# Sketched attention and a gated expert attention on one core: the same jobs in another order

## The chip, the core and the metric

The kernel runs on one core of a Trainium2 chip. The metric is device time in microseconds for one execution, as the median of several; lower is better. The core has five engines that work beside each other, each through its own queue in a fixed order: TensorE (matmuls, PE in the profile), VectorE (DVE), ScalarE (ACT), GpSimd (POOL) and SyncE (SP, which here only starts DMA transfers). An instruction that waits for a semaphore stops everything behind it in its engine's queue.

## What is computed

Two blocks, one after the other, in float32, for 4 batches (`b`) of 1088 positions. Cut to what matters:

```python
# block 1, per batch and head (4 heads of 32)
a, b = x @ S1.T, x @ S2.T                  # 8 sketches each, for q and for k
phi  = outer(a, b)                         # 64 features
kv, z = phi(k).T @ v, phi(k).sum(0)
x = (phi(q) @ kv) / (phi(q) @ z + 1e-6)    # heads side by side: x is 1088 x 128
# block 2: 4 experts, the best 2 of them per position
logits = x @ w_gate
w = softmax over the best 2 logits
for e in experts:
    s = causal((x @ wq[e]) @ (x @ wk[e]).T / 8)
    out += w[e] * softmax(s) @ (x @ wv[e]) @ wo[e]     # where e is among the best 2
```

## The kernel before, in words

The kernel does not walk through loops at run time. It first makes a list of 1275 jobs (`job(...)`, line 79 on): each has a name, one or two engines that it may run on, the values that it reads and makes, the buffers that it holds, and a function that issues its instructions. The constant `ORDER` then names every job once, by its number; a letter behind the number chooses the engine (`a` the first, `b` the second; for the dummy matmuls that warm TensorE up, `b` leaves them out). `Plan.run` (line 85 on) takes the words one after the other:

```python
for word in order:
    n, a = (int(word[:-1]), "ab".index(word[-1])) if word[-1] in "ab" else (int(word), 0)
    j = self.jobs[n]
    ...
        for h in j["holds"]:
            if h not in self.where:
                self.where[h] = free[h[0]].popleft()
        j["f"](j["eng"][a])
```

So `ORDER` decides three things: how the instructions of each engine stand in its queue, which of two engines does a job, and which buffer of a pool a value gets (the one longest free). The framework adds the semaphore waits that the data and the buffers need. Costs written beside the jobs (`us`, `landing`, `rank`) do nothing at run time; the order was found with them outside this file. `mode` is the tile shape in which a job uses TensorE's array: F for 128 x 128 tiles, V for 32 x 128, Q for 32 x 32, M for 128 x 64, L for 128 x 32, and two more for small jobs.

The jobs by stage, with the names that the prediction uses and their lines in the profile:

- Start: 6 dummy matmuls (line 248, two each); loads of S1, S2, q, k, v and the weights; `decode` (303 to 315, VectorE) makes float32 of the sketch matrices, whose inputs come as float64, and `spread1` to `spread3` copy them to the four blocks of 32 partitions.
- Block 1 of batch 0: `turn q0.x` and `turn k0.x` (transposes, 485 and 481); `sketch q0`, `sketch k0` (TensorE, 516); `back ...` (VectorE transposes out of PSUM, 520); `features ...` (products of two sketches, 525, on VectorE or GpSimd); `turn qf` (TensorE, 590), `sums 0.m` (556), `numer 0.m` (613), `divide` (620 to 622), `turn x` (628), `keep x`. Later batches use other steps of the same kind (`sketch`, `back`, `weigh q`, `invert q`, `scale q`, `features`, `turn f`, `numer`, 734 to 768), prepared while the batch before is in block 2. `repeat S2` (352) is a small TensorE job for them.
- x goes to DRAM (`store x`, 640 and 645 for batch 0) and comes back in another layout (`fetch x`, 649 and 786) as weights for the later sums.
- The choice of experts: `logits` (806), `choose a`, `choose b` (831 to 847, small comparisons of two SBUF operands on VectorE), `turn choice` (885, 887), `shares` (GpSimd, 865 to 881); masks for three groups of columns go through DRAM (`store masks`, `fetch masks`, 891 and 896), those of the very first group come by `widen` and `keep mask`.
- Block 2 goes by 3 groups of 64-row steps (6, 6 and 5 steps of 17; a step takes 64 positions with the two experts chosen). Per group: `query` (TensorE, 959), `base` and `pick` (972). Per step i: `score b.i` (997), `take` (adds the mask and finds the maximum, VectorE, 1009), `exp` (ScalarE, 1025), `guard` (1031 or 1033), `invert` (1036), `weigh` (GpSimd, 1040), `turn A` (VectorE transpose, 1045). Per group again: `sum` (TensorE, 1073), `keep V`, `patch V` (1096), `spread V` (GpSimd, 1100), `out` (1144, 1170, 1194), `turn out`, `keep out`, `store out`.

All TensorE results pass through 4 PSUM buffers of two banks (`pair0` to `pair3`), so a score waits until an earlier `take` or `keep` has read the buffer that it gets. Copies (line 192) can run on ScalarE or VectorE.

Of the kernel before, what the change touches and what calls it, by code (L numbers as in the profile page):

```python
# [21 lines left out]
0 3 45 1 42a 16a 8a 5a 22a 26b 2 46 77 7b 48 49 88 76 4 52 51 74 75 56 21a 87 85 86 50 96 78 98 101b 79 53 102a 82 97  # L22
100b 99a 54 64 89 90 27b 81 80 10b 84b 65 92b 66 83a 393 394 91 95b 67a 107 108a 60 111 392 93a 115 109 116a 113 19b
103 112a 13b 110a 63 114a 94a 104 58 391 402 401 405 406 408a 407 395 404 106a 105a 29b 121 122 399 117 118 398 125
123 126 44b 119 403 55 400 397 57 120a 124b 127 685 396 128a 687 59 61 62a 68 70 409a 686 148 131 410a 149 150 146 151
167 147 69 168 411a 152 153 170 154 412 413 414a 684 694 155 132 130 415 133 179 129 171 172 135 180 183a 24b 416 417
420b 418b 419b 162 695 184a 163 164 156 157a 158 159a 181 12b 182 421 185 186 187 194 422 423 47 195 196 424 425 246
188 201 430 426 165 166a 71 202 169 245 431 197a 73 198 189 190b 199 191 192 432 427a 428b 72 215 216 200 250a 174
433a 247 222 249a 251 223 224 225a 208 209 203 193 217 434a 210 211b 25b 248 318 319 322a 252 175 429 160 226 204a 173
689 260 261 691 227 435 212 213 161a 690 253 254 323a 324 14b 214 228 176 218a 219 220 140 436 255 688 437a 136 438a  # L30
205 206 698 699 700 704a 177 320 207 267 256a 702a 134 321 325 221 268 262 263a 264 178a 265 269 270 697 284 283 285
701a 291 292 293 456 458 137 229 230 271a 286 231 141 294 235a 234a 696 287b 295a 257 703b 457 258 272 692 273 693 705
461 459 460 296 31b 232a 236 297 706 143 233b 707a 275 708 462 238 709 710 711a 463 288 289 276 237 239 259 712a 266
277 342 274 278 343 344 144 345 298 279b 280 290 281 713a 714 715 717 716 723 346a 347 348 327 326 38b 328 472 473 329
282 724 725 476a 718 477b 464 478 467 719 350 351 352 726a 353 439 299 300 330b 331 332 727a 349 301 139 138 302 303
304 308a 333 441 142 354a 307b 306b 9b 17b 35b 335 310 474 440 334 305b 309 475 336 479 359 337 338a 358 360 339 361
362 355 468 508 509 442 720a 984 311 312 540 721a 363 340 501 364a 443 502 480 979 341 481 482 541 314 465 487 365 488
356 357 483a 315 313 366 367 538 494 977 978 495 980 316a 981 728 539 542a 368 369 370 987 496 503 504a 145 371 372
373 374 317 469 375 470 543a 544 545 471a 505 506 985 988 484 485 486 497b 444 498 722 499 510 511b 489 490a 491 512
513 376 379b 447 500 380a 515 383 516 553 377a 381 445 554 492 493 378a 382 448 584 585 586 517 518a 729 555 449 446  # L40
453 982 983 730a 514 519 731b 451 991 520 521 993 749 556b 992 994b 587 588a 569 546 996b 750 384 385 997a 507 557 558
547 751 548 386 568 989 522 589 523 524 549a 550 551 559 570 571 526a 752 753 590 242 591 525a 754 611 529 995a 530
241 528b 527a 531 612 616a 561 760 732 452 387 615a 755 455 466 733 572a 756 560 573 574 389 614 562 563 986 613 240
576 577 617 618 620 575 43b 552 532 644 619 578 28b 18b 579 621 243a 580b 581 643 765 652 564a 565 766 769a 582 651
768 757 645 583 636 566 567 390 653 770a 771 635 654 655 627 622 244 623a 761 762 628 637 656 657b 629 630 638 767 772
624 658 659 646 625 592 660 639a 640 631b 641 593 594 450 595 596 597 794 598a 999 647a 632 642 601b 602 648 600a 599a
795 633 634 649 998 736 1000a 603 605 535 626 454 773 774 787 650 534 763 788 533 780 781 808 809 810 811a 764a 536b
812 661 662 789 775 663 813 796 797b 798 790b 604 782 664 665 666 667 1002 814 668 669 990 1005a 734 776b 777 672a
671a 778 1006b 670b 1001 735 739 1003 832 1004a 791 388 799 783b 800 673a 674 675 831 835a 801 784 1007 802 803 1008
792 676 1009 793 836a 834 677 1010 1016 833 904 738 678 742 758 804b 1011 837 30b 1017 785 805 806 759 1012 1018 838  # L50
1013a 905 908a 862 1014a 1020a 909a 807 679 910 878 786 779 737 537 877 879 747 839 840 841 907 906 880 911 861 863
1019a 1021 881b 842a 846 847 682 740 815 816 817 746 864 865a 820a 853 866 867 821a 824 854 1015 868 882 936 819a 823
855 39b 34b 40b 41b 848 849b 937 818a 850 851 856 822 938 1022 1024b 869 1023b 607 843 883 884 939 870 748 871 872
1042 857b 1044 928 680 741 681 844 845 1043 858 606 873a 874 929 608 1045 825 1047 852 930 940a 1046 1048 875 859 860
921 944 945 946 920 743 941 609a 922 610 744 913 931 932a 1049 912 914 947 933 934 942 915 948 876 949 950b 1131 916a
# [1228 lines left out]
```

## Time and profile before

| | |
|---|---|
| Time, median of 3 runs | 273.25 us (273.1 to 274.25) |
| Span of the profiled execution | 272.5 us |
| TensorE busy | 261.4 us, 4081 matmul instructions |
| VectorE busy | 215.1 us |
| GpSimd busy | 153.9 us |
| ScalarE busy | 102.0 us |
| HBM traffic over the span | 98 GB/s |

The span runs from the first to the last instruction; the rest of a run's time lies around it. A float32 matmul appears as two instructions. TensorE's ends are modelled and overlap the next start, so spacing between starts says more than a duration. In the timeline a line has its start, the time to the end of the last of the merged instructions, engine, line of the kernel, operation, what it writes and reads, shape, count, and in brackets the idle time ahead of it with what ended that. Lines of the DMA view have the count, the size and the median time from issue to landing.

### The profile page before, as it was taken

How to read it: one execution, taken by the hardware profiler on the slowest of the kernel's cores; microseconds unless marked ns; L12 is line 12 of the kernel's file. 1: busy time of each engine (PE TensorE's matmuls, PEld its weight loads, DVE VectorE, ACT ScalarE, POOL GpSimd, SP SyncE). 2: the span in 40 equal slices, each digit the busy share in tenths (PEclk: the TensorE clock that was granted, in tenths of full speed). 3: DMA queues.
4: the chain of work that ended last, by engine and by line, in shares of the span. 5: the costliest groups of instructions: out<-in, count | busy, mean ns of one | idle time of the engine just before them, and what ended most of it. 6: DMA issues, size and time to landing. Idle time of an engine off the chain costs nothing.

```text
span 272.5 us, 9727 instructions
## 1 busy us (share of the span) xinstructions
PE 261.4 (96%) x4081; PEld 194.4 (71%) x4081; DVE 215.1 (79%) x534; ACT 102.0 (37%) x274; POOL 153.9 (56%) x248
## 2 busy tenths in 40 slices
PE   7789999989999999989999999999999999999994
PEld 2578754557596895766599976756696975789994
DVE  4878789889999879998968438999899368995244
ACT  2052346643423517143552341453433335334110
POOL 3498179757679545545574558565448342653640
PEclk9999999999999999999999999999999999999999
DMA  6869569921638979045700166601502755830012
GB/s 203 144 129 148 124 124 179 194 30 30 132 65 141 210 183 165 17 89 108 162 6 4 38 146 153 159 1 39 110 2 71 140 119 119 168 76 2 5 31 53
DMA packets 80588, 27.38 MB, mean 100 GB/s; under 512 B 49760, under 2 KB 79520, under 8 KB 80544
## 3 DMA queue, kind: packets, MB, share of 16 engines
q1 hardware_dynamic: 80096, 26.10, 49.0%
q8 instruction: 32, 0.52, 0.8%
q10 hardware_dynamic: 448, 0.66, 0.7%
q14 instruction: 12, 0.10, 0.1%
HBM read 22.22 MB, written 4.52 MB: 98 GB/s over the span
## 4 chain that ended last, share of the span: by engine, by line
PE 73%; DVE 14%; DMA 6%; issue 3%; ACT 1%; POOL 1%; SPq 1%; DVEq 0%
PE pair L1073 27%; PE pair L997 21%; PE pair L959 8%; PE pair L1194 6%; PE pair L556 2%; DMA xra<-xd 2%; PE pair L1144 2%; DMA in<-in_k_dram 2%; DVE fp L525 2%; DVE w L520 2%; PE pair L516 2%; DVE w L1009 1%; DVE AT L1045 1%; PE pair L1170 1%; PE pair L756 1%
## 5 line engine op out<-in xcount | busy, mean ns | idle before, releaser
L1040 POOL TENSOR_SCALAR w<-w,rs,sh 128x384 f32<-128x384 f32 (+15 forms) x68 | 56.9, 844 | 56.2 <-DVE rs L1036 53.9
L1025 ACT ACTIVATE w<-w,mx 128x384 f32<-128x384 f32 (+15 forms) x68 | 52.4, 771 | 72.0 <-DVE mx L1009 64.8
L997 PE MATMUL pair<-xT,qs 128*128 128x384 f32 (+11 forms) x216 | 76.1, 480 | 2.8 <-DVE agg L192 1.3
L997 PEld LDWEIGHTS pair<-xT,qs 128*128 128x128 f32 x216 | 37.7, 190 | 28.8 <-issue 10.7
L1045 DVE STREAM_TRANSPOSE AT<-w 128x576 f32<-128x576 f32 (+15 forms) x68 | 50.9, 759 | 6.1 <-POOL w L1040 5.5
L1009 DVE CUSTOM_DVE_ANT_0 w<-pair,mask 128x768 f32<-128x768 f32 (+14 forms) x68 | 48.2, 719 | 6.4 <-PE pair L997 5.9
L1073 PEld LDWEIGHTS pair<-AT,xra 32*128 32x128 f32 x1136 | 41.3, 185 | 5.8 <-DVE mx L1009 2.6
L1073 PE MATMUL pair<-AT,xra 32*128 32x160 f32 (+5 forms) x1136 | 44.2, 302 | 0.0
L1100 POOL TENSOR_TENSOR agg<-agg,mb 128x768 f32<-128x768 f32 (+1 forms) x22 | 34.1, 1560 | 10.7 <-ACT agg L192 4.5
L959 PE MATMUL pair<-xT,Mq 128*128 128x384 f32 (+1 forms) x96 | 35.0, 477 | 0.1
L525 POOL TENSOR_TENSOR fp<-w 128x576 f32<-128x576 f32 x24 | 28.9, 1219 | 6.9 <-DVE w L520 6.9
L192 ACT COPY agg<-pair 128x384 f32<-128x384 f32 (+1 forms) x32 | 13.7, 461 | 42.1 <-PE pair L1073 34.5
L1073 PE MATMUL pair<-AT,xrb 32*128 32x160 f32 (+5 forms) x752 | 26.8, 287 | 0.1
L1073 PEld LDWEIGHTS pair<-AT,xrb 32*128 32x128 f32 x752 | 26.1, 185 | 0.7 <-issue 0.7
L972 DVE COPY_PREDICATED qs<-mb,pair 128x768 f32<-128x768 uint16 (+1 forms) x24 | 23.1, 961 | 2.6 <-DMA mb<-md 1.3
L959 PEld LDWEIGHTS pair<-xT,Mq 128*128 128x128 f32 x96 | 17.2, 190 | 10.4 <-issue 2.5
L1194 PEld LDWEIGHTS pair<-Mo,agg 128*128 128x128 f32 x168 | 20.6, 192 | 2.4 <-issue 1.3
L1194 PE MATMUL pair<-Mo,agg 128*128 128x128 f32 x168 | 21.6, 278 | 0.0
L192 DVE COPY agg<-pair 128x384 f32<-128x384 f32 (+1 forms) x14 | 7.5, 536 | 12.7 <-PE pair L1073 7.5
L1036 DVE RECIPROCAL rs<-rs 128x1 f32<-128x1 f32 x68 | 8.9, 141 | 8.1 <-POOL rs L1033 6.3
L1033 POOL TENSOR_SCALAR rs<-zs 128x1 f32<-128x1 f32 x30 | 6.4, 214 | 15.7 <-ACT w L1025 12.8
L1096 DVE COPY_PREDICATED agg<-mb,pair 128x384 f32<-128x384 uint16 (+1 forms) x24 | 12.7, 547 | 3.2 <-ACT agg L192 3.0
(159 smaller groups left out, 307.5 us busy)
## 6 DMA issues: line engine op xcount, KB each, us to landing
mb<-md SPq DMA_DIRECT2D x7, 576.0 KB, 5.3
xra<-xd SPq DMA_DIRECT2D x16, 192.0 KB, 4.8
xrb<-xd SPq DMA_DIRECT2D x16, 192.0 KB, 4.1
xrc<-xd SPq DMA_DIRECT2D x16, 160.0 KB, 4.1
mb<-md SPq DMA_DIRECT2D x4, 480.0 KB, 5.4
in<-in_k_dram SPq DMA_DIRECT2D x12, 136.0 KB, 4.2
in<-in_q_dram SPq DMA_DIRECT2D x3, 544.0 KB, 5.6
xd<-w SPq DMA_DIRECT2D x12, 136.0 KB, 3.5
```

What stands on the lines that cost most here:

```text
L192: (nc.scalar.copy if eng == "ACT" else VEC[eng].tensor_copy)(o, i)
L525: VEC[e].tensor_tensor(out=f, in0=a[:, :, None, R : 2 * R].to_broadcast([128, NJ, R, R]), in1=a[:, :, 0:R, None].to_broadcast([128, NJ, R, ...
L959: nc.tensor.matmul(plan[ps[x]][:, y, 0:w], Mq[:, ((1, 2), (0, 3))[x][y]], plan[xT][:, 64 * t0 : 64 * t1], start=True, stop=True)
L972: nc.vector.copy_predicated(chosen(), rows(c), rows(plan[ps[x]]))
L997: nc.tensor.matmul(plan[p][:, y, 0 : c1 - c0], plan[qs][:, 128 * t : 128 * t + 128], plan[xT][:, c0:c1], start=True, stop=True)
L1009: nc.vector.tensor_tensor_reduce(out=o, in0=src, in1=msk, scale=-1.0, scalar=mx[:, b, i, x - 1 : x] if x else 3e38, op0=ALU.add, op1=ALU.m ...
L1025: nc.scalar.activation(out=a, in_=a, func=ACTF.Exp, bias=mx[:, b, i, last : last + 1], scale=-1.0, accum_out=zs[:, b, i : i + 1])
L1040: nc.gpsimd.tensor_scalar(out=a, in0=a, scalar1=rs[:, b, i : i + 1], scalar2=plan[("sh", b)][:, i : i + 1], op0=ALU.mult, op1=ALU.mult)
L1045: nc.vector.transpose(dst[:, 0 : keys // 32, t], plan[A][:, 0:keys].rearrange("p (j s) -> p j s", s=32))
L1073: nc.tensor.matmul(plan[Vk[g // 2]][:, g % 2, lo : 32 * nt], plan[(f"xr{j // 12}", b)][rows, j % 12], a[rows, j, lo:], start=(j == 0), sto ...
L1100: nc.gpsimd.tensor_tensor(out=a, in0=a, in1=plan[mb][:, 2 * x : 2 * x + 2, 0:w], op=ALU.mult)
L1194: nc.tensor.matmul(plan[p][0:m, 0, 128 * x : 128 * x + 128], plan[agg][:, e, 128 * x : 128 * x + m], Mo[:, e], start=(e == 0), stop=(e == ...
```

## The change

Only `ORDER` is replaced. The jobs, their instructions and their sizes stay; every job is still there once, with the same six pairs of dummy matmuls. The first and last lines of both lists:

```diff
 ORDER = """
-0 3 45 1 42a 16a 8a 5a 22a 26b 2 46 77 7b 48 49 88 76 4 52 51 74 75 56 21a 87 85 86 50 96 78 98 101b 79 53 102a 82 97
-100b 99a 54 64 89 90 27b 81 80 10b 84b 65 92b 66 83a 393 394 91 95b 67a 107 108a 60 111 392 93a 115 109 116a 113 19b
...
-1260 1262a 1100 1195 1264a 1085 1196 1197 1199 1263b 1261a 1265 1266 1268 1198 1072 1086 1108 1109 1267 1200a 1201
-1110 1115b 1116 20b 1269 1111a 23b 1113 1112 1119 1114b 1270 1273 1271 1117 1118b 1274 1120 1121 1122 1272 1127b 1128b
-1123b 1124a 1125b 1126a 36b
+0 3 1 76 2 79 77 87 45 5a 48 4 75 78 8a 22a 42a 74 88 16a 56 51 21a 86 60 50 46 80 54 49 81 85 52 53 96 82 97 89 98 59
+57 392 90 101a 61 65 393 62a 66 100b 391 102a 91 99b 18b 64 83a 94a 111 115 67a 84a 116a 95a 92b 394 93a 58 109 107 113
...
+1267 1198 1111a 1268 1200a 1112 1201 1113 1269 1115a 974 1116 1114a 1117 1119 1118b 1120 13b 1121 1270 1122 1271 1273
+1127b 1274 1125a 1272 1126b 1128a 1123a 1124b
 """.split()
```

By names, the engines' queues at the places that the prediction speaks of (old above new):

```
SP, start
 old  load S0, q0.0, w0, k0.0, w4, v0.0, v0.1, w1, v0.4, w2, v0.3, v0.2 ...
 new  load q0.0, S0, v0.1, v0.0, k0.0, w4, v0.2, w2, v0.3, w0, w1, v0.4 ...
VectorE, start
 old  decode, turn q0.1, spread3, turn q0.0, turn k0.0, turn k0.1, back q0.1, features q0.3, back q0.0,
      features q0.0, back k0.0, back k0.1, features k0.1, features k0.2, turn k1.1, turn k1.0, back k1.0 ...
 new  turn q0.0, decode, turn q0.1, spread3, turn k0.1, turn k0.0, back q0.0, back q0.1, back k0.0, features q0.2,
      features q0.3, back k0.1, features k0.2, features k0.3, features k0.1, turn k1.1, turn k1.0, keep sums 0.0 ...
GpSimd, start
 old  features q0.2, features q0.1, spread v1, features k0.0, features k0.3, pick8, onehot, rep4, features k1.0 ...
 new  rep16, gate order, features q0.1, features q0.0, features k0.0, rep4, onehot, features k1.3 ...
TensorE, start
 old  sketch q0, turn w0, sketch k0, turn w1, turn w2, turn qf, sums 0.0, sums 0.1, sketch k1, numer, turn x, repeat S2 ...
 new  sketch q0, sketch k0, repeat S2, turn w1, turn w2, turn w0, turn qf, sums 0.1, sums 0.0, sketch k1, numer, turn x ...
SP, around the stores of x
 old  ... load k2.1, v1.0, k2.3, k2.2, store x 0.2, load k2.0, store x 0.3, 0.1, 0.4, 0.0, store masks 0, fetch masks 0.1 ...
 new  ... load k2.2, k2.0, k2.3, store x 0.4, 0.2, 0.3, 0.1, 0.0, load k2.1, fetch x 0.02, store masks 0, fetch x 0.12 ...
VectorE, around sum 1.0
 old  ... take 1.9.0, choose a2.0, choose b2.0, turn A 1.11, maximum 2.0, patch V 1.0.0, patch V 1.0.1, keep V 1.0.1 ...
 new  ... take 1.9.0, choose a2.0, maximum 2.0, take 1.6.0, back k3.0, choose b2.0, base 1.2.1, pick 1.2.0 ...
```

Of the 1241 jobs that are issued, 86 change engine: 5 go from VectorE to GpSimd and 4 the other way (7 of these 9 are feature products), 21 copies go from VectorE to ScalarE and 16 the other way, 37 `guard` and spread jobs change between ScalarE and GpSimd, and three stores of the last group change between SP and ScalarE. TensorE's 314 jobs have 65 changes of tile shape between neighbours in the new list, 69 in the old.

More of the change, by code (lines that the diff above doesn't have):

```diff
@@ L27 @@
[L27 to L55, printed above, removed]
-917 951 1130 1053 918 1054 1129 1133b 935 1025 1132 923 952 885 886 943 887 888 889 890 1134a 1051 891a 1135 1136 892b
```

56 lines of the change are left out of this document (43 added, 13 removed).

## The prediction

> **What bounds the kernel now.** I read the page's first part, then the windows by stage, then TensorE's timeline around its gaps, and last what VectorE and GpSimd did there.
>
> ```profile
> span 272.5 us, 9727 instructions
> PE 261.4 (96%) x4081; PEld 194.4 (71%) x4081; DVE 215.1 (79%) x534; ACT 102.0 (37%) x274; POOL 153.9 (56%) x248
> ```
>
> ```profile
> 0.00:20.00 20.00, 16.36 (x400) 10.05 (x403) 14.09 (x31) 6.13 (x12) 11.29 (x29) 1.00 0.71 162
> 20.00:37.00 17.00, 16.52 (x284) 12.62 (x279) 14.04 (x49) 5.26 (x13) 9.18 (x22) 1.00 0.66 118
> 37.00:57.00 20.00, 18.11 (x196) 10.16 (x183) 18.12 (x51) 11.41 (x36) 16.99 (x34) 1.00 1.10 171
> 57.00:92.00 35.00, 35.00 (x524) 25.44 (x523) 32.77 (x82) 13.32 (x35) 26.16 (x34) 1.00 0.47 89
> 92.00:124.00 32.00, 30.68 (x566) 23.86 (x565) 28.93 (x70) 13.10 (x39) 15.50 (x26) 1.00 0.64 126
> 124.00:262.00 138.00, 137.69 (x2048) 106.28 (x2050) 102.56 (x243) 52.28 (x141) 73.86 (x108) 1.00 0.37 80
> 262.00:272.50 10.50, 7.01 (x98) 5.96 (x90) 4.56 (x11) 0.48 (x1) 0.88 (x1) 1.00 0.23 55
> ```
>
> The columns are TensorE, its weight loads, VectorE, ScalarE and GpSimd, then clock, DMA share and GB/s. TensorE is the bound: from 57 us to 262 us it idles 1.6 us in all, and the granted clock is 1.00 throughout. Its jobs are the same in both lists, so an order can win only four things: waits (3.6 us of idle before 20 us, 1.9 us between 37 and 57, 1.3 us between 92 and 124), the cost of tile shape changes, work placed where TensorE waits anyway, and the end. VectorE is a close second from 20 to 92 us, with 64.9 us busy of 72.
>
> **The price of a shape change.**
>
> ```profile
> 86.78 0.81 PE L959 MATMUL pair<-xT,Mq 128*128 128x384 f32 x2
> 87.42 0.76 PE L997 MATMUL pair<-xT,qs 128*128 128x256 f32 x4
> 143.15 0.70 PE L997 MATMUL pair<-xT,qs 128*128 128x256 f32 x2
> 143.78 2.29 PE L556 MATMUL pair<-vp,fp 128*64 128x33 f32 x72
> ```
>
> Modelled ends overlap, so I take start to start. A 384-column pair among its like is 0.64 us, so 256 columns are 0.43. The score at 143.15, with a change before and a change behind it, takes 0.63: half of each change falls into it, so one change is 0.2 us.
>
> **TensorE's list against its time.** The spacing of each kind of job, where it waits for nothing, summed over the two lists, with 0.2 per change:
>
> ```profile
> 24.85 0.82 PE L628 MATMUL pair<-ident,w 128*128 128x128 f32 x6
> 58.99 3.18 PE L1073 MATMUL pair<-AT,xra 32*128 32x192 f32 x92
> 266.10 2.92 PE L1170 MATMUL pair<-Mo,agg 128*128 128x128 f32 x24
> ```
>
> From the last numerator of batch 0 (ended 24.85) to the first `sum` (58.99) the old list holds 27.5 us of jobs and 19 changes, 31.3 us; it took 34.1, so 2.8 us are waits. From there to the last output block (266.10) it holds 196.7 us and 43 changes, 205.3; it took 207.1, so 1.8 us are waits. The new list holds 28.2 us with 21 changes (32.4) and 195.4 us with 38 changes (203.0). Together 236.6 becomes 235.4: **-1.2 us**, of which 0.6 are three changes saved here (69 to 65 over the whole list) and 0.6 is `repeat S2`, which moves ahead of the numerators into time in which TensorE waits for features. If that cover were gone, its 0.6 would come back.
>
> **The wait at 119.9 us.**
>
> ```profile
> 114.78 1.68 POOL L1040 TENSOR_SCALAR w<-w,rs,sh 128x448 f32<-128x448 f32 x2 [1.21 <-DVE rs L1036]
> 115.94 0.59 DVE L831 TENSOR_TENSOR ch<-ch 128x34 f32<-128x34 f32 x1
> 116.42 1.18 POOL L525 TENSOR_TENSOR fp<-w 128x576 f32<-128x576 f32 x1
> 116.45 1.23 DVE L832 TENSOR_TENSOR ch<-ch 128x34 f32<-128x34 f32 x1
> 117.80 0.21 DVE L835 TENSOR_TENSOR ch<-ch 128x34 f32<-128x34 f32 x1
> 120.60 0.54 DVE L192 COPY agg<-pair 128x384 f32<-128x384 f32 x1
> 121.19 1.24 PE L997 MATMUL pair<-xT,qs 128*128 128x288 f32 x4 [1.32 <-DVE agg L192]
> ```
>
> `choose a2.0` on VectorE has two instructions that take 0.59 and 1.23 us instead of 0.21, each ending where a GpSimd instruction ends: GpSimd holds VectorE for 1.4 us. Everything behind in VectorE's queue is late by that, the copy at 120.60 (`keep V 1.0.1`) last, and TensorE waits 1.32 us for the PSUM that it frees. The new list gives that copy to ScalarE, puts `choose a2.0` behind another `take`, and puts score 1.8 before `sum 1.0.0`. Late next is `sum 1.0.0`: from score 1.9.00 to it, back, choices, base and two picks keep VectorE 6.2 us against 5.8 us of TensorE work, 0.4 us short. Net **-0.9** (0 if a new hold falls there, -1.3 if none).
>
> **Up to the numerators.**
>
> ```profile
> 2.88 0.17 DVE L303 TENSOR_SCALAR w<-w 32x32 int32<-32x32 int32 x1 [1.62 <-DMA w<-in_S_dram]
> 4.18 0.23 DVE L315 STREAM_TRANSPOSE SK<-w 32x64 f32<-32x64 f32 x1
> 5.74 0.78 DVE L485 STREAM_TRANSPOSE in<-in 128x576 f32<-128x576 f32 x1 [1.33 <-DMA in<-in_q_dram]
> in<-in_q_dram SPq DMA_DIRECT2D x1, 256.0 KB, 3.5
> 6.58 0.77 PE L516 MATMUL pair<-in,SK 32*32 32x32 f32 x64
> 7.54 1.50 PE L516 MATMUL pair<-in,SK 32*32 32x256 f32 x64 [0.19 <-DVE in L485]
> 12.75 1.43 DVE L520 STREAM_TRANSPOSE w<-pair 128x576 f32<-128x576 f32 x2
> 14.06 2.31 POOL L525 TENSOR_TENSOR fp<-w 128x576 f32<-128x576 f32 x2
> 14.11 3.54 DVE L525 TENSOR_TENSOR fp<-w 128x576 f32<-128x576 f32 x2
> 41.05 0.74 DVE L525 TENSOR_TENSOR fp<-w 128x576 f32<-128x576 f32 x1
> ```
>
> The new list loads q0.0 first on SP (issue at about 1.0, landing 3.5 later, 4.5) and puts `decode` (13 instructions, 2.88 to 4.4, so 1.5 us) behind its turning: 4.5 + 0.7 + 1.5 + 0.8 for `turn q0.1` + 0.2 for the spread lets the first sketch begin at 7.7 instead of 6.6. The two v loads put ahead of k0.0 on SP make k0.0 later too, but by 10.1, when this sketch (2.4 us) ends, it need not be there before. The next sketch then runs straight on, in PSUM of its own, to 12.4; so `back k0.0` starts at 12.4, not 12.75. Behind it stand five feature products on VectorE (one more than was there) and a turning: 0.72 + 5 x 0.74 + 0.7 = 5.1, done at 17.5 if nothing holds them; in the old list they were done at 17.65, with 3.54 us for two, 2.1 over the free price. GpSimd now runs its three products, the copies of rep4 and the one-hot beside them, so a hold is likely here: between none and two products (2.3 us). I take one, 1.15, against the 0.2 won: **+0.9** (-0.2 to +2.2).
>
> The Trainium skill (SBUF — State Buffer, Who interferes with whom) says that a VectorE instruction with two SBUF inputs and a GpSimd instruction that reads SBUF exclude each other for a whole instruction, whichever starts first. By that alone a hold ends with the GpSimd instruction in flight, and the sum would be the one I take; the row at 14.11 waited for two in a row, and by that row it would be 1.2 us worse.
>
> **From the numerators to the first sum.**
>
> ```profile
> 26.13 1.99 SPq L640 DMA_DIRECT2D xd<-w  x1
> 30.91 0.42 SPq L640 DMA_DIRECT2D xd<-w  x1
> in<-in_k_dram SPq DMA_DIRECT2D x12, 136.0 KB, 4.2
> 34.75 2.18 DVE L972 COPY_PREDICATED qs<-mb,pair 128x768 f32<-128x768 uint16 x2
> 36.62 6.97 SPq L440 DMA_DIRECT2D vp<-in_v_dram  x3
> 37.13 1.45 DVE L520 STREAM_TRANSPOSE w<-pair 128x576 f32<-128x576 f32 x2 [0.21 <-PE pair L516]
> ```
>
> The last load of k2 moves behind all stores of x on SP. These ran from 26.13 to 31.3 with one load among them; without it they end at 30.8, and the load lands 4.2 later, at 35.0. `turn k2` waits for it, and on VectorE's queue stand behind it the first picks, `back q1` and the first takes: 35.0 + 1.5 + 2.2 + 0.2 + 1.45 + 0.5 for `take 0.4.0` is 40.8. Score 0.1.00 needs that take's PSUM; TensorE's work ahead of it since 24.85 is 14.4 us, 39.3. So the new list waits 1.5 us there; the chains behind it, to `sum 0.0.0`, are shorter than TensorE's work. With 0.1 for the rest, 2.8 becomes 1.6: **-1.2** (-2.2 to +1.0).
>
> **Elsewhere** no chain of the new list between TensorE steps is more than 0.2 us longer than TensorE's work beside it; but many are only just shorter, so I keep 0 with -0.5 to +1.5. The end (turn out, three copies, stores split otherwise over ScalarE and SP) has the same number of steps: 0, within 0.3.
>
> **Sum**: -1.2 - 0.9 + 0.9 - 1.2 = -2.4; 272.5 - 2.4 = 270.1. The median of the runs shown, 273.25, is 0.75 above the span, so the forecast is **270.8 us**.
>
> **The rivals.** *Held twice at the start*: the feature products lose 2.3 us to GpSimd and the wait at 119.9 shrinks by half only; +1.1 and +0.5 make it 272.4. For it speaks the row at 14.11, against it that two of GpSimd's three products can run there before VectorE's first is ready. *No holds at all*: the start gains 0.2 instead of losing 0.9, the wait at 119.9 goes whole (-1.3), and the sum is -3.9, 269.3. For it: VectorE hands five copies more to ScalarE than it gets back, 2.7 us less work at the 0.54 of the row at 120.60; against it: one feature product more at the start. *SP's queue sticks* (the slower side): at 36.62 three loads kept SP for 6.97 us. If the new list's queue sticks so before the last k2 load, which now lies behind five stores, that load lands up to 5.5 us later (7.0 less the 1.4 that the first store already shows above the others), and VectorE and TensorE with it: 270.8 + 5.5 - 0.5 of waits swallowed is 275.8. It decides from 3.8 us of lateness on. Against it: the old queue was free again by 28.2. *The change buys nothing*: the changes saved are real, but chains with no slack give it back; 273.0.
>
> **How the numbers follow.** Forecast 0.47, no holds 0.15, held twice 0.16, nothing bought 0.10, queue sticks or another slower end 0.12. Half a per cent, about what a measurement can tell here, is 1.4 us: faster is below 271.9, slower above 274.6. Forecast (its own range 269.8 to 272.1, nine tenths faster) and no holds make 0.58 faster; the rest of the forecast, held twice and nothing bought 0.30; slower 0.12. The range reaches from the best bounds that come together (268.4) to most of the queue's case (274.8).
>
> **What would show it.** Right: TensorE's idle time in 92 to 124 us below 0.6; the first numerators ending between 24.6 and 27; VectorE's `L831`/`L832` near 0.2 us; TensorE's first `sum` near 59.8 (58.99 + 0.9 - 1.2, and 1.1 more work ahead of it). Wrong: `L525` on VectorE far above 0.74 before 20 us, a VectorE wait for k2's load longer than 2 us, or new TensorE idle behind 124 us, where the old list has 0.3.

## The result, and the profile after

| | before | after |
|---|---|---|
| Time, median (20 runs each) | 273.37 us | 275.91 us |
| Ratio, 95% interval | | 1.009 [1.0069, 1.0111] |
| Span of the profiled execution | 272.5 us | 273.9 us |
| Time of the profiled execution | not told | 275.64 us |

The new order is slower by 2.5 us; forecast were 270.8 us, between 268.4 and 274.8. In all 20 runs of the changed kernel the time is 1.7 to 1.8 us above the span. The clock below is the granted TensorE clock, as a share of full speed. The page of the kernel after, its first part:

```profile
span 273.9 us, 9738 instructions
PE 263.2 (96%) x4081; PEld 197.0 (72%) x4081; DVE 210.4 (77%) x528; ACT 104.7 (38%) x280; POOL 156.2 (57%) x248
```

The same stretches as before, of the kernel after (length, then TensorE, its weight loads, VectorE, ScalarE, GpSimd, clock, DMA share, GB/s):

```profile
0.00:20.00 20.00, 16.14 (x296) 10.46 (x296) 13.07 (x30) 6.22 (x12) 11.69 (x33) 0.84 0.75 167
20.00:37.00 17.00, 16.75 (x316) 13.82 (x316) 12.70 (x48) 5.48 (x15) 7.16 (x13) 0.99 0.59 111
37.00:57.00 20.00, 19.87 (x252) 11.36 (x251) 19.61 (x51) 11.06 (x34) 16.18 (x34) 1.00 1.00 166
57.00:92.00 35.00, 34.71 (x514) 24.49 (x514) 33.40 (x85) 14.44 (x38) 26.26 (x35) 1.00 0.63 122
92.00:124.00 32.00, 31.20 (x573) 23.86 (x572) 23.37 (x66) 13.07 (x39) 15.60 (x30) 1.00 0.43 82
124.00:262.00 138.00, 136.43 (x2082) 105.93 (x2080) 104.92 (x246) 52.50 (x141) 76.53 (x106) 1.00 0.42 82
```

Three things catch the eye. Before 20 us the clock is 0.84 (1.00 before) and TensorE got 296 matmuls done instead of 400. From 20 to 57 us TensorE no longer waits: 0.4 us of idle time against 2.4. Behind 57 us its idle time is larger, 2.7 us against 1.6, and most of that is behind 124 us (1.6 against 0.3), where I had forecast none.

TensorE's timeline of the kernel after, from the dummies to `turn qf` (its number of matmuls is behind the x, the idle time ahead of it in brackets):

```profile
1.31 5.30 PE L247 MATMUL pair<-idle 128*128 128x512 bf16 x12 [1.31 <-DVE idle L240]
6.82 3.14 PE L515 MATMUL pair<-in,SK 32*32 32x32 f32 x211 [0.20 <-DVE in L484]
12.30 1.33 PE L515 MATMUL pair<-in,SK 32*32 32x256 f32 x45 [2.34 <-issue]
13.56 1.06 PE L351 MATMUL pair<-ident,rep 32*128 32x32 f32 x4
14.55 1.54 PE L379 MATMUL pair<-ident,AT 128*128 128x128 f32 x6
15.88 4.31 PE L589 MATMUL pair<-ident,fp 128*128 128x128 f32 x18
```

In the middle of the second sketch, at 10 us, TensorE stops for 2.34 us, and the reason given is "issue": it waits for nothing that the profile shows. No semaphore stands there. What ends shortly before is a DMA that no instruction of the kernel starts. The DMA view of before between 8.5 and 9 us:

```profile
q1 hardware_dynamic: 66, 0.02, 26.0%
q8 instruction: 1, 0.02, 18.0%
```

and of after between 9.5 and 10 us (between 6 and 9.5 us it has no such line, and q1 is at 113.8%):

```profile
q1 hardware_dynamic: 403, 0.09, 126.4%
q8 instruction: 1, 0.02, 16.3%
```

Over the whole run of the kernel after, this queue shows:

```profile
q8 instruction: 32, 0.52, 0.8%
```

That is 32 pieces of 16 KB for the 8162 instructions that the page counts on TensorE (4081 matmuls and as many weight loads), 255 to a piece: I take q8 for the queue of TensorE's own instructions. In the new list the piece begins a us later, with the DMA engines full of the kernel's loads (q1's packets take 126% of that half microsecond, 26% before). It takes 1.3 us (16.3% of 16 engines' half microsecond), and TensorE goes on about 1.4 us behind its end. Since it now does both sketches in one run, TensorE gets to the place where it stops 1.6 us sooner than in the old list: it stops behind a matmul that began at 9.6, and the old list began that one at 11.2 us.

Behind the stop the clock falls. Windows of the kernel after:

```profile
12.00:14.00 2.00, 1.70 (x47) 1.12 (x47) 0.83 (x2) 0.00 (x0) 0.04 (x1) 0.89 1.01 160
14.00:20.00 6.00, 6.00 (x27) 5.32 (x27) 5.97 (x6) 4.50 (x9) 5.57 (x6) 0.50 0.50 134
20.00:22.00 2.00, 2.00 (x61) 1.88 (x62) 1.71 (x3) 0.00 (x0) 0.00 (x0) 0.90 0.00 0
```

0.89, 0.50 and 0.90 make half clock from 13.6 to 20.4 us, 6.8 us long; the 18 matmuls of `turn qf` take 4.31 us in it. The Trainium skill (TensorE: Matmul & The Clock Gate, Part 1) has the gate pass half of the pulses after an idle window of about 3.4 us. The half clock is there, twice as long as that; but TensorE stood still for only 2.34 us.

VectorE and GpSimd of the kernel after, beside it:

```profile
13.17 0.78 DVE L519 STREAM_TRANSPOSE w<-pair 128x576 f32<-128x576 f32 x1 [2.85 <-PE pair L515]
13.88 2.37 DVE L524 TENSOR_TENSOR fp<-w 128x576 f32<-128x576 f32 x2
16.98 3.45 DVE L524 TENSOR_TENSOR fp<-w 128x576 f32<-128x576 f32 x3
14.03 1.60 POOL L524 TENSOR_TENSOR fp<-w 128x576 f32<-128x576 f32 x1 [1.99 <-DVE w L519]
15.58 2.31 POOL L343 COPY rep<-ident 32x128 f32<-32x128 f32 x4
17.96 1.86 POOL L367 CAST AT<-ident 64x1536 bf16<-64x1536 f32 x1
```

`back k0.0` waits 2.85 us for the sketch. The five feature products behind it take 2.37 + 3.45 = 5.82 us where 5 x 0.74 = 3.70 were free: they are held by GpSimd for 2.1 us, all along `features k0.0`, `rep4` and `onehot`. They end at 20.4, the moment at which `turn qf` at half clock ends too (20.2): the two delays lie side by side.

**Stage by stage**, on the spans (starts of the first `turn x`, of the first `sum` and of the last output block; the fourth line is the run of the old start with the new rest, the last the kernel before, profiled again):

| | to turn x | to first sum | to last out | to the end | span |
|---|---|---|---|---|---|
| before | 24.85 | 34.14 | 207.1 | 6.4 | 272.5 |
| forecast | 25.75 | 34.05 | 203.9 | 6.4 | 270.1 |
| after | 28.05 | 31.83 | 207.1 | 6.9 | 273.9 |
| old start, new rest | 24.79 | 32.52 | 207.1 | 7.1 | 271.5 |
| before, again | 24.86 | 33.06 | 207.0 | 6.5 | 271.4 |

### The profile page after: what moved, and what is told of

Same layout as the page of the kernel before. It is cut to its first block, busy times and chain, and to the rows that moved or that the text cites. A ratio compares the mean times of both kernels' runs of the same rounds, so it can differ in the third digit from the quotient of the medians.

```text
span 273.9 us, 9738 instructions
## 1 busy us (share of the span) xinstructions
PE 263.2 (96%) x4081; PEld 197.0 (72%) x4081; DVE 210.4 (77%) x528; ACT 104.7 (38%) x280; POOL 156.2 (57%) x248
## 4 chain that ended last, share of the span: by engine, by line
PE 85%; DVE 7%; issue 2%; ACT 2%; DMA 2%; POOL 1%; ACTq 0%; DVEq 0%; POOLq 0%
PE pair L1072 27%; PE pair L996 24%; PE pair L958 9%; PE pair L1193 6%; PE pair L515 5%; PE pair L1143 3%; PE pair L555 3%; DVE AT L1044 2%; DMA in<-in_q_dram 2%; PE pair L612 2%; PE pair L589 1%; PE pair L805 1%; DVE qs L971 1%; ACT agg L191 1%; DVE agg L1095 1%
## 5 line engine op out<-in xcount | busy, mean ns | idle before, releaser
L1039 POOL TENSOR_SCALAR w<-w,rs,sh 128x64 f32<-128x64 f32 (+14 forms) x68 | 56.0, 829 | 53.2 <-DVE rs L1035 45.9
L996 PE MATMUL pair<-xT,qs 128*128 128x320 f32 (+11 forms) x216 | 75.1, 479 | 2.3 <-DVE qs L971 0.7
L1024 ACT ACTIVATE w<-w,mx 128x768 f32<-128x768 f32 (+16 forms) x68 | 52.4, 771 | 49.4 <-DVE mx L1008 42.2
L1072 PEld LDWEIGHTS pair<-AT,xra 32*128 32x128 f32 x1136 | 42.4, 185 | 4.5 <-DVE AT L1044 1.2
L1072 PE MATMUL pair<-AT,xra 32*128 32x160 f32 (+5 forms) x1136 | 45.1, 302 | 0.0
L524 POOL TENSOR_TENSOR fp<-w 128x576 f32<-128x576 f32 x25 | 29.5, 1195 | 12.1 <-DVE w L519 11.7
L1072 PEld LDWEIGHTS pair<-AT,xrb 32*128 32x128 f32 x752 | 26.7, 185 | 0.2 <-issue 0.2
L191 ACT COPY qs<-pair 128x384 f32<-128x384 f32 (+1 forms) x20 | 8.8, 463 | 17.5 <-PE pair L958 17.4
L515 PE MATMUL pair<-in,SK 32*32 32x288 f32 (+2 forms) x544 | 12.5, 356 | 2.7 <-issue 2.3
```

The source lines that it names most:

```text
L191: (nc.scalar.copy if eng == "ACT" else VEC[eng].tensor_copy)(o, i)
L515: nc.tensor.matmul(dst if early else dst.rearrange("p (j t) -> p j t", t=32), SK[rows, 1] if s else first_[rows], part(src[rows], g), star ...
L524: VEC[e].tensor_tensor(out=f, in0=a[:, :, None, R : 2 * R].to_broadcast([128, NJ, R, R]), in1=a[:, :, 0:R, None].to_broadcast([128, NJ, R, ...
L996: nc.tensor.matmul(plan[p][:, y, 0 : c1 - c0], plan[qs][:, 128 * t : 128 * t + 128], plan[xT][:, c0:c1], start=True, stop=True)
L1024: nc.scalar.activation(out=a, in_=a, func=ACTF.Exp, bias=mx[:, b, i, last : last + 1], scale=-1.0, accum_out=zs[:, b, i : i + 1])
L1039: nc.gpsimd.tensor_scalar(out=a, in0=a, scalar1=rs[:, b, i : i + 1], scalar2=plan[("sh", b)][:, i : i + 1], op0=ALU.mult, op1=ALU.mult)
```

## The experiments

Each ratio is to runs of the kernel before on the same chip; it is an estimate over the single executions and not the quotient of the medians, so where executions spread the two differ. The kernel before against itself gave 1.0027 (below), so a third of a per cent is not told apart by times alone. Each kernel was profiled in one execution only; what is read from its timeline holds for that one.

**Which part of the list costs.** Two halves, joined at the last `turn x` of batch 0:

```diff
 e1: order = old[:112] + [w for w in new if w not in old[:112]]
 e2: order = new[:110] + [w for w in old if w not in new[:110]]
```

> The old list's first 112 words (up to the last turn x of batch 0), then the rest in the new list's order. Theory A (the start costs: TensorE ran out of instructions at 10 us in the new list because the two sketches of 256 small matmuls each stand next to each other, and the idle window then halved its clock): no idle time of TensorE over 1 us before 20 us, granted clock 1.00 from 7 us on, numerators of batch 0 done at 25.0 +- 0.4 instead of 28.2, first sum between 57.0 and 58.8 instead of 59.9, time 1.5 to 2.8 us below the changed kernel's 275.9. Rival B (the start's lateness is swallowed later, the loss stands in the new list's many small waits behind 60 us): numerators at 25 too, but first sum at 59.5 to 60 and a time within 0.6 us of 275.9.

Measured: 273.37 us, 0.9976 [0.9955, 0.9997]. The first `turn x` begins at 24.79, the first `sum` at 57.31, the clock is 1.00.

> The new list's first 110 words (up to the last turn x of batch 0), then the rest in the old list's order. Theory A: the gap of 2.3 us at 10 us and the half clock from 13.6 to 20.4 us are there again, numerators done at 28.2, first sum between 60 and 61.5 instead of 59.0, time 0.8 to 2.2 us above the kernel before (274.2 to 275.6). Rival B: the same gap and clock, but the first sum at 59.0 to 59.5 and a time within 0.6 us of the kernel before.

Measured: 276.77 us, 1.0097 [1.0062, 1.0131]. The gap is there again (TensorE's timeline of e2):

```profile
7.33 3.14 PE L515 MATMUL pair<-in,SK 32*32 32x32 f32 x211 [0.72 <-DVE in L484]
12.00 1.33 PE L515 MATMUL pair<-in,SK 32*32 32x256 f32 x45 [1.53 <-issue]
```

So the start makes the whole loss, 2.5 us with the new rest and 3.2 with the old one (1.2 us beyond what I gave it, and its first sum, at 62.3, is later than I gave it too; why the old rest makes it dearer is not shown). The rest of the new list is worth 0.2% by the ratio and nothing by the medians (273.37 against 273.52 beside it), less than the kernel before differs from itself: theory A holds, and rival B is right in that the new rest does not win what it should.

**Is it code that TensorE waits for?** The dummy matmuls are cut smaller, so that more instructions stand ahead in TensorE's queue:

```diff
-nc.tensor.matmul(plan[h][:, 0], idle[:, 0:128], idle, start=True, stop=True) for _ in range(2)]
+nc.tensor.matmul(plan[h][:, 0, 0:128], idle[:, 0:128], idle[:, 0:128], start=True, stop=True) for _ in range(7)]
```

> The new list; each of the six dummy jobs issues 7 matmuls of 128 columns instead of 2 of 512, so TensorE's queue holds 60 instructions more ahead of the first sketch, in about the same time. If TensorE's gap at 10 us is a wait for instructions (theory A), it is tied to the place in TensorE's instruction stream: it begins 15 float32 matmuls (30 matmul records) earlier in the second sketch, 0.2 to 0.4 us sooner, and the third piece of code starts to load that much sooner too. If it is a wait for k0's data or for VectorE (rival C), the gap ends at the same matmul of the second sketch as in the changed kernel. Time within 0.8 us of 275.9 by both.

Measured: 276.04 us, 1.0082 [1.0054, 1.011]. TensorE's timeline of e3:

```profile
1.31 4.66 PE L247 MATMUL pair<-idle 128*128 128x128 bf16 x42 [1.31 <-DVE idle L240]
6.90 3.62 PE L515 MATMUL pair<-in,SK 32*32 32x32 f32 x181 [0.92 <-DVE in L484]
12.59 1.96 PE L515 MATMUL pair<-in,SK 32*32 32x32 f32 x57 [2.08 <-issue]
```

42 + 181 = 223 matmuls stand ahead of the gap, as 12 + 211 = 223 in the changed kernel and in e2. The gap moved by exactly the 30 records, to a matmul that in the changed kernel ran without a wait. That speaks against data, PSUM and the other engines, which stand at places in the data: the gap stands at a place in TensorE's code. One part of the expectation failed: the piece did not load sooner (it began at 10.0) and the gap did not begin sooner, since the first sketch itself came a little later; so it is not the using up of the earlier code alone that sets the piece's time.

**Filling the gap.** Four dummies more between the sketches:

```diff
-... sketch q0, load v0.4, back q0.0, sketch k0 ...
+... sketch q0, load v0.4, back q0.0, dummy, dummy, dummy, dummy, sketch k0 ...
```

> The new list with four more dummy jobs (eight bf16 matmuls of 512 columns, 0.21 us each at full clock, 1.7 us together) between the two sketches. Theory A: the code comes at the same time, so the second sketch still ends at 13.6 +- 0.4, but TensorE's idle time is only 0.5 to 1.2 us, the clock stays 1.00, the 18 matmuls of turn qf take 2.4 us instead of 4.3, and the numerators are done at 26.6 +- 0.5; if that reaches the end, the time is 274.3 to 275.3, by rival B 275.5 to 276.2. Rival C (data): the gap keeps its length and stands 1.7 us later, numerators no earlier than 28.

Measured: 276.97 us, 1.0113 [1.007, 1.0156]. TensorE's timeline of e4:

```profile
1.31 4.20 PE L247 MATMUL pair<-idle 128*128 128x512 bf16 x12 [1.31 <-DVE idle L240]
6.73 2.04 PE L515 MATMUL pair<-in,SK 32*32 32x32 f32 x128 [1.22 <-DVE in L484]
8.70 2.13 PE L247 MATMUL pair<-idle 128*128 128x512 bf16 x8
10.76 1.21 PE L515 MATMUL pair<-in,SK 32*32 32x32 f32 x75
12.31 1.40 PE L515 MATMUL pair<-in,SK 32*32 32x256 f32 x53 [0.35 <-issue]
16.75 2.22 PE L589 MATMUL pair<-ident,fp 128*128 128x128 f32 x17 [1.56 <-DVE fp L524]
```

12 + 128 + 8 + 75 = 223 again, and the next matmul at 12.31, as with the gap unfilled: the code came no sooner. The second sketch ended at 13.6, the clock stayed at 1.00 and `turn qf` took 2.2 us, as expected. The time was not: 277.0 us lies above both ranges. Nor were the numerators done at 26.6, but at 28.1, as in the changed kernel: at full clock TensorE now waits for VectorE's products. So the half clock alone cost nothing that shows at the numerators; the hold lay beside it. The executions of the changed kernel say the same: the three whose mean clock over the run was 0.992 or more took 275.2 to 275.8 us, in the middle of the others (275.0 to 277.6), as far as that record is complete (see the last section).

**The hold.** `rep4` and `onehot` behind GpSimd's products of k1, with the four dummies (e7) and without (e8):

```diff
-... features k0.0, rep4, onehot, features k1.3, k1.2, k1.0, k1.1 ...
+... features k0.0, features k1.3, k1.2, k1.0, k1.1, rep4, onehot ...
```

> The new list with the four dummy jobs between the sketches (clock kept) and with GpSimd's rep4 and onehot moved behind its feature products of k1, so that they no longer run beside VectorE's five feature products. If VectorE's products were held by these GpSimd instructions: L524 on VectorE 0.74 to 0.85 us each before 20 us (1.16 in the changed kernel), the numerators of batch 0 done at 26.4 +- 0.5 instead of 28.1, and a time 0.8 to 2 us below the run with the dummies alone (277.0). If the products are not held by them, no change: 28.1 and 276.5 to 277.4.

> The new list with only GpSimd's rep4 and onehot moved behind its feature products of k1; code wait and half clock as in the changed kernel. If the hold and the half clock are two delays of the same length side by side (TensorE's turn qf at half clock until 20.2 us, VectorE's products until 20.4): VectorE's products are done near 18.5, but the numerators end at 27.8 to 28.3 as before and the time stays within 0.6 us of 275.9. If the hold alone sets the end of the start: numerators at 26.5 and a time 1 to 2 us below 275.9.

Measured: e7 275.83 us, 1.0078 [1.0051, 1.0105]; e8 276.13 us, 1.0105 [1.0071, 1.014]. VectorE's timeline of e7:

```profile
14.04 2.37 DVE L524 TENSOR_TENSOR fp<-w 128x576 f32<-128x576 f32 x2
17.14 2.10 DVE L524 TENSOR_TENSOR fp<-w 128x576 f32<-128x576 f32 x3
```

The group of three takes 2.10 us instead of 3.45: `rep4` and `onehot` had held it for 1.35. The first two are still held, by the one GpSimd product that runs beside them. With both delays away (e7) the numerators end at 26.6 and the time is 1.1 us below e4's, as expected; with the hold alone away (e8) the time stays that of the changed kernel (its profiled execution, at 279.0 us, was the slowest of nine; its numerators, at 28.9, are not read further). That is what two delays side by side would give. But e7 is no faster than the changed kernel, though its numerators end 1.5 us sooner: half of that is gone at the first `sum` (59.12 against 59.88, with a wait of 1.0 us for a `turn A` between), and where the four dummies cost the rest is not shown.

**Why the code came late.** The new list with SyncE's first loads in the old order (q0.0 stays first):

```diff
-SP: load q0.0, S0, v0.1, v0.0, k0.0, w4, v0.2, w2, v0.3, w0, w1, v0.4, k1.1, k1.2, k1.0, k1.3
+SP: load q0.0, S0, w0, k0.0, w4, v0.0, v0.1, w1, v0.4, w2, v0.3, v0.2, k1.2, k1.3, k1.1, k1.0
```

> The new list with SyncE's first 16 loads (and their order alone) as in the old list, except that q0.0 stays first. TensorE's order is the new one. If the piece of code that TensorE waits for comes late because it queues behind the data that the new list asks for sooner (its load began at 9.1 to 10.0 us in the runs with the new start, 8.6 to 9.3 with the old), it begins 0.3 to 1.0 us sooner here, record 224 of the matmuls starts at 11.2 to 11.8 us instead of 12.0 to 12.6, and the time is 0.3 to 1 us below 275.9. If the loads have nothing to do with it, the code's load begins at 9.1 to 10.0 and the time stays within 0.4 of 275.9.

Measured: 274.68 us, 1.0039 [1.0019, 1.0058], 1.2 us below the changed kernel and a little more than I gave it. In its DMA view between 8 and 8.5 us:

```profile
q1 hardware_dynamic: 166, 0.04, 74.5%
q8 instruction: 1, 0.02, 16.9%
```

The piece begins a us sooner, the next matmul behind the 223 starts at 11.2 instead of 12.3, and all that follows is 1.1 us sooner (`back k0.0` at 12.09 instead of 13.17, the first `turn x` at 26.99 instead of 28.05). That the loads set the piece's time fits all traces, if not tightly: it began at 9.1 to 10.0 us in the six with the new loads (the changed kernel, e2, e3, e4, e7, e8) and at 8.1 to 9.2 in the eleven others. e9 moves 16 loads at once; which of them counts is not shown. No gap behind 223 matmuls is left in e9: what TensorE waits for now is k0, ahead of the second sketch, and the clock still falls, from 11.8 us on (TensorE's timeline and a window of e9):

```profile
9.86 3.13 PE L515 MATMUL pair<-in,SK 32*32 32x32 f32 x128 [1.27 <-DVE in L480]
12.00:14.00 2.00, 2.00 (x18) 1.13 (x15) 1.91 (x3) 0.00 (x0) 2.00 (x3) 0.50 1.12 176
```

**The other 1.3 us.** On e9's list: the clock kept and the hold away (e13: two dummies behind the first sketch, in PSUM of their own; `rep4`, `onehot` as above), the hold away alone (e14), the clock kept alone (e15).

> The new list with the old order of SyncE's first loads, two dummy jobs (0.85 us) right behind the first sketch, in PSUM that nobody else holds, and rep4 and onehot behind GpSimd's products of k1: neither half clock nor hold. If these two, side by side, are the rest of the start's cost: clock 1.00, numerators of batch 0 done at 25.3 to 26.0 us (27.0 with the old loads alone, 25.0 before), time 273.5 to 274.1 (274.7 with the old loads alone). If something else in the new start costs, numerators at 26.5 or later, 274.4 to 274.9.

> The new list with the old order of SyncE's first loads, and rep4 and onehot behind GpSimd's products of k1; the clock falls as before. Side by side: turn qf at half clock keeps TensorE until 19.2 us whatever VectorE does, numerators at 26.7 to 27.2, time 274.4 to 275.0. If the hold alone sets the end of the start: as with both undone (25.3 to 26.0, 273.5 to 274.1).

> The new list with the old order of SyncE's first loads, and two dummy jobs right behind the first sketch; VectorE's products beside rep4 and onehot. Side by side: clock 1.00, but VectorE's products are done only at 19.6 to 20 us and the sums wait for them; numerators at 26.3 to 27.2, time 274.2 to 275.0. If the clock alone sets the end of the start: as with both undone.

| on the old loads | half clock | full clock |
|---|---|---|
| held | e9: 274.68, 1.0039 [1.0019, 1.0058] | e15: 274.78, 1.0046 [1.0018, 1.0074] |
| not held | e14: 275.54, 1.0039 [1.0007, 1.0071] | e13: 274.13, 1.0008 [0.9986, 1.0031] |

Either alone brings nothing in the median; both together bring the kernel back to where the kernel before is, as far as times can tell. The step is 0.3%, no more than the kernel before showed against itself, and in e13's profiled execution (275.47 us, the slowest of its 12) the numerators are done at 26.4, not at 25.3 to 26.0. e14 is 0.5 us above what I gave it, and its numerators, at 27.9, are 0.7 later; e15 lies in its range, but its profiled execution took 288.3 us and is not read.

The single executions say more than the medians. The mean clock of each is on record; 6.8 us at half clock in 274 make it 0.988. Three of e14's executions kept 0.994 or more and took 273.1 to 273.5 us; eight with 0.978 to 0.992 took 274.8 to 277.0 (one more, with 0.932, took 288.2). So with the hold away the lost clock goes with some 2 us, and with the hold there (the changed kernel above, or e9 beside e15) with little: in e9 the two executions with 1.00 and 0.994 took 273.8 and 274.0, the ten others, at 0.988 or less, 274.3 to 275.6; but e15, eleven of whose 13 executions have 0.990 or more, is no faster than e9. That clock and hold side by side are the rest fits; its size is not settled. An earlier try with three dummies (e11, and e12 with the moves told below) put a new wait in:

> The new list with the old order of SyncE's first loads, three dummy jobs (1.3 us) between the two sketches, where TensorE now waits 1.3 us for k0, and GpSimd's rep4 and onehot behind its feature products of k1. If the loss of 2.5 us is made of the code that came late behind the loads (1.2 of it by the run with the old loads), and of the half clock and the hold of VectorE side by side (the rest), all of it is undone: clock 1.00 from 6 us on, L524 on VectorE 0.7 us each in its group of three, numerators of batch 0 done at 24.6 to 25.4 us, first sum at 57.2 to 58.2, time 273.0 to 273.9. If something else in the new start costs, numerators at 26 or later and 274.3 to 275.

> The run beside it, with the moves of the mended kernels behind the start (turn A 3.6, keep V 2.0.2, keep V 0.2.3, the last copies and stores, turn out 3.2; not repeat S2, which the new list has early). If those moves are worth the same 0.9 to 1 us on the new start as on the old, 0.7 to 1.1 us below the run beside it, 272.0 to 272.9; if they only showed on the old start, the same as the run beside it.

Measured: 275.66 us (1.0065 [1.0037, 1.0093]) and 274.65 us (1.0013 [0.9984, 1.0042]). Both are 1.8 us above the time that I gave them. The third dummy got the PSUM of the first sketch, waited 1.41 us for `back q0`, and k0's sketch began at 11.4. e11's profiled execution has clock 1.00 before 27 us and the numerators done at 26.6, but it took 274.0 us, the second fastest of 12, and what makes the others slower is not shown: the run neither bears the account out nor speaks clearly against it. e12 beside e11 is 1.0 us lower, so the moves may be worth as much on the new start; the two intervals overlap.

**What span belongs to the time.**

> The kernel before itself, for the span of a typical execution. The prediction took its 272.5 us span as belonging to the median of 273.25 (0.75 us around the span). If instead the same 1.7 us lie around the span as in the changed kernel, spans here are near 271.7 to 271.9 and the profiled execution of before was a slow one by 0.8 us; if the prediction's reading holds, spans are 272.6 to 272.8 with 0.75 us around them.

Measured: 274.49 us (10 runs; 31 others of the same kernel beside it 273.45; 1.0027 [1.0002, 1.0052]); profiled span 271.4 at 273.09 us, so 1.7 us lie around the span of the kernel before too. The profiled execution of 272.5 us on which I built was one of 274.2 us, 0.8 above the median. TensorE's idle time from 37 to 57 us, 1.9 us in it, is 0.8 us in this one.

**Are the small waits real?** TensorE's waits of the kernel after between 57 and 262 us (us in total, times, longest):

```profile
PE pair L996 <- DVE qs L971: 0.7, 1, 0.7
PE pair L996 <- DVE agg L1095: 0.7, 1, 0.7
PE pair L996 <- DVE rs L1035: 0.5, 1, 0.5
PE pair L696 <- ACT kvr L191: 0.3, 1, 0.3
```

The third ends at 105.8 us. VectorE's timeline of the kernel after just before it:

```profile
104.60 0.49 DVE L191 COPY agg<-pair 128x320 f32<-128x320 f32 x1 [2.37 <-ACT agg L191]
105.30 0.47 DVE L1095 COPY_PREDICATED agg<-mb,pair 128x320 f32<-128x320 uint16 x1
```

`keep V 0.2.3` on VectorE does nothing until ScalarE has finished `keep V 0.2.1`, which reads the same PSUM buffer; `patch V` comes behind it, and the score behind that, because it needs the buffer (the profile names the `invert`, L1035, that VectorE does right behind `patch V`). On e1's list:

```diff
-keep V 0.2.2/ACT, keep V 0.2.1/ACT, keep V 0.2.3/DVE
+keep V 0.2.2/ACT, keep V 0.2.3/DVE, keep V 0.2.1/ACT
-keep V 2.0.3/ACT, keep V 2.0.0/ACT, keep V 2.0.1/ACT, keep V 2.0.2/DVE
+keep V 2.0.2/DVE, keep V 2.0.3/ACT, keep V 2.0.0/ACT, keep V 2.0.1/ACT
-turn A 3.6, pick 3.2.0, pick 3.2.1
+pick 3.2.0, pick 3.2.1, turn A 3.6
-turn x 0.2, gate order, rep16, repeat S2
+gate order, rep16, repeat S2, turn x 0.2
-keep out 3.0.2/DVE, 3.0.1/ACT, 3.0.0/ACT; store out 3.0.1/ACT, 3.0.2/SP, 3.0.0/ACT
+keep out 3.0.2/DVE, 3.0.0/DVE, 3.0.1/DVE; store out 3.0.2/ACT, 3.0.0/SP, 3.0.1/SP
 e10 also:
-mix V 3.0.1, patch V 3.0.1, scale V 3.0.1, turn out 3.2
+mix V 3.0.1, turn out 3.2, patch V 3.0.1, scale V 3.0.1
```

> The old start and the new rest (as in the run with the old list's first 112 words), with six small moves at TensorE's waits behind the start: turn A 3.6 behind pick 3.2.1; keep V 2.0.2 (VectorE) ahead of the three that ScalarE copies; keep V 0.2.3 (VectorE) ahead of keep V 0.2.1 (ScalarE); repeat S2 with rep16 ahead of the last turn x; the three last copies on VectorE with the old list's stores. If the new rest's small waits are what eats the gain forecast for it, these lose 0.7, 0.5, 0.6, 0.5 and 0.5 us: time 270.3 to 272.0 against 273.4 without the moves. If they are only symptoms of engines that are full beside TensorE, the waits reappear a few us later and the time stays within 0.6 of 273.4.

> The mended kernel of the run before (old start, new rest, six moves) with one move more: the turning of out 3.2 stands ahead of the last two VectorE steps of the last sums, so that its four stores leave SyncE before the last two stores come. In the mended kernel these two were issued at 268.0 us, 0.5 us behind their copies. If SyncE's queue is what holds the end, the last stores go 0.4 us sooner and the time falls by 0.2 to 0.6 to about 272.1; if the last output block then waits for VectorE instead, no change (272.5).

Measured: e6 272.53 us, 0.997 [0.9948, 0.9991]; e10 272.41 us, 0.9961 [0.9938, 0.9984]. e6 falls between its two ranges, and e10 shows no step beside it. In e10 VectorE's copy runs beside ScalarE's first one, which reads another PSUM buffer; ScalarE's second, on the same buffer, now begins at 101.46, when VectorE's has ended (ScalarE's and VectorE's timeline):

```profile
100.89 1.00 ACT L191 COPY agg<-pair 128x320 f32<-128x320 f32 x2 [6.68 <-PE pair L1072]
100.93 0.49 DVE L191 COPY agg<-pair 128x320 f32<-128x320 f32 x1 [1.62 <-PE pair L1072]
101.92 0.51 DVE L1095 COPY_PREDICATED agg<-mb,pair 128x320 f32<-128x320 uint16 x1 [0.21 <-ACT agg L191]
```

and the longest of TensorE's waits between 57 and 262 us are 0.3 us each:

```profile
PE pair L996 <- DVE qs L971: 0.3, 1, 0.3
PE pair L696 <- ACT kvr L191: 0.3, 1, 0.3
PE pair L996 <- DVE agg L1095: 0.3, 1, 0.3
```

The seven moves together bring 1.0 us by the medians (273.37 to 272.41) and 0.4 by the ratios to the kernel before (0.9976 to 0.9961), whose intervals overlap; either is less than the 2.8 that I had added up for six of them. e10, the old start with the new rest so mended, beats both kernels: 1.2 us below the kernel before that ran beside it, 3.5 below the changed one.

## Why the prediction was wrong

**The step that failed most**, in its own words: "The next sketch then runs straight on, in PSUM of its own, to 12.4". I had asked whether data and PSUM let the two sketches run on without a break, and they do. I had not asked whether TensorE's instructions do. They ran out behind 223 matmuls, the next could be had at 12.3, and the sketch ended at 13.6. The start was forecast 0.9 us later than before and is 3.2 later: by VectorE's chain 0.8 of the missing 2.3 us stand at `back k0.0` (13.17 for 12.4), 1.0 are the hold, and 0.5 come behind the products. The sentences ahead of it were wrong the other way: q0.0 landed at 3.7 us and not at 4.5, so the first sketch began at 6.8 and not at 7.7, and k0.0 was turned a microsecond sooner than before (7.37 against 8.34), not later. That the sketch did not need it earlier was true. The price of the new order of loads was elsewhere, in the code that came late: 1.2 us by e9.

**The hold at the start** was taken as 1.15 us and was 2.1, as in the rival *held twice at the start*. It did not show by itself, since the half clock lay beside it; when the clock was kept (e4 against e7), it did.

**From the numerators to the first sum** I forecast 34.05 us and measured 31.83; with the start undone 32.52. The waits there were overrated twice: 1.1 of the 2.8 us were in that one execution only, and the new list has none left (0.13 us idle from 37 to 57). The load of k2 behind the stores of x never came into play: between 28 and 42 us VectorE's longest wait is 1.5 us, and it is for TensorE. So the rival *SP's queue sticks* falls. The first `sum` stands at 59.88, where I had said 59.8: two errors of 2.3 and 2.2 us that cancel, which is luck and no proof of anything.

**The wait at 119.9 us** went as forecast: L831 and L832 take at most 0.24 us, and the 1.32 us of waiting is gone. But the stretch still idles 0.80 us and not below 0.6, most of it (0.54) in the new wait at 105.8.

**TensorE's list and "elsewhere"** hid the second miss. The list is shorter (the work from the first sum on was counted as 203.0 against 205.3 us), and yet the stretch takes 207.1 us in both. Together with the stretch ahead of it the miss is smaller than its 3.2 us: from the first `turn x` to the last output block I forecast 238.0 us and measured 238.9, since what was counted too low behind the first sum had been counted too high before it. What grew behind it are waits: TensorE idles 2.7 us between 57 and 262 us, 1.6 before. "Elsewhere no chain of the new list between TensorE steps is more than 0.2 us longer" was the step: I took durations on an engine as free of each other, and did not see that a copy on VectorE stands behind one on ScalarE that reads the same PSUM buffer, or that a transpose ahead of two picks delays a score. The four waits shown above make 2.2 us; with three of them cut or gone, and the end mended, 0.4 to 1.0 us came back.

**The rise from span to median** was 0.75 us by my reckoning and is 1.7. I set the span of one execution beside the median of others; by that reckoning the run that had been profiled was the slowest of the three shown. From 270.1 that alone is 1.0 of the 5.1 us by which I missed: 3.8 are the stages above, 0.3 the changed kernel's median above its own profile.

Of the signs, the numerators ended at 28.2 us and not between 24.6 and 27, and two that were to show it wrong came: `L524` on VectorE far above 0.74 us before 20 us (1.16 in the mean), and 1.6 us of idle TensorE behind 124 us. The half clock was not on my list at all: the granted clock had been 1.00 throughout, and I took that for a property of the kernel. It differs by list and even by execution: of 129 executions of the kernel before beside the experiments, 103 had a mean clock of 0.996 or more (median 273.45 us), and six had less than 0.99 (275.4 us).

## What to carry to other kernels

An order that packs many small matmuls together must also be paid for in instructions: count them from the start of the queue, and see in the DMA view when the next piece of code comes and what data transfers are asked for just ahead of it. When two delays lie side by side, taking one away shows nothing; both have to go before either is called harmless. And a forecast that leans on waits of 1 us needs more than one profiled execution, with span and time of the same run.

## What the runs showed of the hardware

TensorE's code comes by DMA in pieces of 16 KB (32 of them, 0.52 MB), while the DMA engines carry the data. In the changed kernel, e2, e3, e4 and e8 the gap stood behind exactly 223 matmuls, whatever they were, and ended 1.3 to 1.5 us behind the end of the piece's transfer. The Trainium skill (Runtime: NRT & Kernel Launch, Instruction fetch mechanics) tells of blocks of 256 instructions, fetched ahead and mostly hidden; the traces agree on the blocks (255 counted instructions to a piece), but with 32 x 32 tiles TensorE used one up in about 1.9 us (the first sketch, 128 matmuls and as many weight loads), and 0.4 to 2.3 us of the fetch were not hidden.

The clock fell to half after TensorE had stood still for 2.34 us, and in e9 for only 1.27 us, in the first 14 us of the kernel; it stayed there for 6.8 us in both. Where dummies filled these gaps (the profiled executions of e4 and e13), it stayed at 1.00. The length of one stop does not decide it: in e7 TensorE stood still for 1.52 and 1.56 us and in e11 for 1.41 and 1.57, and the clock stayed at 1.00 (`turn qf` at full speed in both). What does decide it is not shown. Nor is the record of the clock quite complete: in e3's profiled execution it stays at 1.00 from 4 to 30 us, but the six matmuls of `turn w` behind the gap take 1.54 us, as at half clock in the changed kernel, and not 0.88, as in e4.
